# An RWKV-7 attention and a SoLU feed-forward in one kernel: GpSimd's scalings tied to points in ScalarE's work, a negated norm, shorter inverses, and a later centring of w_out

## The chip, the cores and the metric

The kernel runs on one core of a Trainium2 chip. Its time is device microseconds from the first to the last instruction of one launch with what lies around it. Three runs were timed without the profiler; the profile is of one further execution. A change is read against the median of the timed runs.

The core has five engines with a queue each, which take their instructions strictly in order: PE (TensorE: matmuls and transposes, and its weight loads, PEld), DVE (VectorE), ACT (ScalarE), POOL (GpSimd) and SP (SyncE, which here only issues transfers). ACT and POOL issue transfers too, from their own queues.

## The reference

```python
# attention, for each of 4 x 8 heads; the state is 40 x 40; 768 steps
y[:, :, t] = np.einsum('bhd,bhde->bhe', rt, state)
Sa = np.einsum('bhde,bhe->bhd', state, at)
state = state * wt[:, :, None, :] - np.einsum('bhd,bhe->bhde', Sa, bt) + np.einsum('bhd,bhe->bhde', vt, kt)

# feed-forward, on the 3072 x 320 matrix that the attention leaves
h = x @ w_in                                    # 320 -> 1024
e = np.exp(h - h_max)
solu = h * (e / (np.sum(e) + 1e-09))
ln = (solu - mu) / np.sqrt(var + 1e-06) * g_ln  # mu, var over the 1024
out = ln @ w_out                                # 1024 -> 320
```

The weights come as 64-bit floats, which the kernel takes apart by integer operations.

## The kernel before

**Tiles and slots.** The sequence is cut into chunks of 64 steps; two of the four batches go together, so there are N = 24 pieces of work (12 chunks, 2 pairs), numbered i. The main loop (line 815) runs over slots i = -1 to 27. A slot has work for several pieces at different stages: the preparation of j = i + 5 (`front`, `front_b`, `norm`: 64 x 64 matrices of a against b), the attention of i, and the feed-forward of earlier pieces (m = i - 1; `hidden(m-2)`, `output(m-3)`). Before the loop a hand-written preamble prepares pieces 0 to 3 and most of 4. The order on every engine is the order in which the program is written.

**The inverse.** Within a chunk the recurrence over 64 steps is solved with the inverse of a unit triangular matrix. `norm(j)` builds the matrix `nt` (DVE masks it out of PSUM, L375) and stores it to DRAM from POOL (L401). For every second piece `begin_inverse` starts one inverse for two pieces (16 heads each): `invert` clears a tile `uu` on POOL (L418, L419), loads the blocks of `nt` as `blk` with four POOL transfers (L412), and then yields; DVE goes on with L422 (the tile is the negative of every second row of `blk`), L423 (ones on the diagonal) and thirty steps, each a product (L428) and a subtraction (L430) on small tiles. `some(n)` and `narrow(.., n)` run n such steps at four places of a slot (`shares`). At the end the inverse goes to DRAM (L436), and `bring` (L449, L451) loads it for each piece as `tu` and `uh`. `flip` (DVE, L457) transposes a part of `tu`; then `couple` on PE makes `py` from it, which ACT copies as `wy` with the factor -1 in the lower half (L469), and `close` makes `pz`.

**Masks.** DVE masks four results of PE in a slot, from PSUM: `psi` and `lv` at its start (after `solved` and `scores`), `nt` and `lu` in its middle, all on L375; between them comes `aT` (L366).

**GpSimd's scalings.** `scaled(j+1)` multiplies b and k of piece j + 1 by the inverse decay (L337, two instructions of 128 x 320). It stands behind `flip` and `highest` in the program, but POOL goes ahead as soon as its queue allows. In front of it in POOL's queue are the loads of r (L280) and the update of the state (L638), behind it the six transfers of `left` (L648, L650), then the store of `nt` (L401), `rs` (L701) and, in every second slot, the start of an inverse.

**The mean of w_out.** The layer norm's mean is taken out of the weights once: `mean_of` (PE, L229) sums the rows of `w2` in slots 2 and 3 as its parts arrive, and `centred(mean)` (DVE, L236, two instructions) subtracts it from `w2` in slot 4, before the first half of the first `output`.

**Other places that the change touches.** In `leave` the state's new value is added up by DVE (L634); for the first piece of each pair, in slots 0 and 1, it is a copy (L636). In the preamble `decay(5)` (ACT logarithm L316, a PE matmul L325, two ACT exponentials) stands behind `some(14)`, which ends the first inverse and issues its store, and behind `scores(0)`.

Of the kernel before, what the change touches and what calls it, by code (L numbers as in the profile page):

```python
# [10 lines left out]
I32 = mybir.dt.int32  # L11
# [17 lines left out]
def shape_constants():  # L29
    s, t = np.arange(P)[:, None], np.arange(P)[None, :]  # L30
    same = s // C == t // C
    row = np.arange(P)[:, None] % C
    parts = dict(
        ident=np.eye(P),
        cum=same & (s <= t),
        tri=row < np.arange(C)[None, :],
        eye_hi=row == Q + np.arange(Q)[None, :],
        neg_hi=-(row >= Q).astype(np.float64),
        mean=np.full((P, P), 2.0 ** -10),
    )  # L40
# [8 lines left out]
def kernel(  # L49
# [46 lines left out]
    def c_(name):  # L96
        lo, hi = where[name]
        return cst[:, lo:hi]
# [124 lines left out]

    def mean_of(lo, hi, begun=None):
        t = bank("pmean")
        if begun is not None:
            nc.tensor.matmul(t[:, 0:DM], lhsT=ident, rhs=begun, start=True, stop=False)
        for c in range(lo, hi):
            nc.tensor.matmul(t[:, 0:DM], lhsT=c_("mean"), rhs=w2[:, c, :], start=begun is None and c == lo, stop=c == hi - 1)  # L229
        mean = two.tile([P, DM], FP32, tag="osb", name="mean", bufs=1)  # L230
        nc.scalar.copy(out=mean, in_=t[:, 0:DM])
        return mean

    def centred(mean):
        for x in range(0, NF, NF // 2):
            nc.vector.tensor_tensor(out=w2[:, x:x + NF // 2], in0=w2[:, x:x + NF // 2],  # L236
                                    in1=mean.unsqueeze(1).to_broadcast([P, NF // 2, DM]), op=ALU.subtract)
# [92 lines left out]
    def scaled(i, names="bk"):  # L330
# [4 lines left out]
        for n in names:  # L335
            j = H * (n == "b")
            nc.gpsimd.tensor_tensor(out=kb[:, j:j + H, 0:D], in0=d["raw_" + n], in1=heads(d["inv"]), op=ALU.mult)  # L337

    def turned(name, x):
        t = bank("p" + name)  # L340
        for j in range(4):
            nc.tensor.transpose(out=t[0:W2, j * P:(j + 1) * P],  # L342
                                in_=x[:, 2 * j:2 * j + 2].rearrange("p a b -> p (a b)")[:, 0:W2], identity=ident)
        return t[0:W2].rearrange("p (j b t) -> p b j t", j=4, b=2)
# [3 lines left out]

    def kept(name, t, bufs=1):
        o = tokens(name, bufs)  # L350
        nc.scalar.copy(out=o[0:W2], in_=t)
        return o
# [15 lines left out]
    def front_b(i):  # L368
        if not ok(i):
            return  # L370
        d = st[i]
        d["bT"] = kept("bT", turned("b", d["kb"][:, H:]))

# [41 lines left out]
    def invert(n):  # L415
        u = two.tile([P, Q // 2, Q], FP32, tag="uu", name="uu")
        flat = u.rearrange("p c t -> p (c t)")
        nc.gpsimd.memset(u[C:P], 0.0)  # L418
        nc.gpsimd.memset(flat[C:P, 1::Q + 2], 1.0)  # L419
        nb = spread(n)  # L420
        yield
        nc.vector.tensor_scalar(out=u[0:C], in0=nb[0:C, 0::2], scalar1=-1.0, scalar2=None, op0=ALU.mult)  # L422
        nc.vector.memset(flat[0:C, 0::Q + 2], 1.0)  # L423
        for j in range(1, Q - 1):
            m, n_c = Q - 1 - j, (j + 1) // 2
            prod = two.tile([P, Q * Q // 8], FP32, tag="prod", name="prod", bufs=1)
# [3 lines left out]
            nc.vector.tensor_tensor(out=u[:, 0:n_c, j + 1:Q], in0=u[:, 0:n_c, j + 1:Q], in1=t, op=ALU.subtract)  # L430
# [28 lines left out]
    def couple(i):  # L459
# [4 lines left out]
        for u in in_turn(lambda p, q, g, h: (p ^ h, p)):  # L464
# [4 lines left out]
        nc.scalar.activation(out=wy[:, :, :, 0:Q], in_=t[:, :, 0:4 * Q].rearrange("p h (j c) -> p h j c", j=4),  # L469
                             func=AF.Copy, scale=c_("neg_hi"))  # L470

# [138 lines left out]
    def leave(i):  # L610
# [21 lines left out]
        for q in range(2):  # L632
            if ci:
                nc.vector.tensor_tensor(out=tot[0:W2, q::2], in0=y[:, q, :, C:], in1=old[:, q::2], op=ALU.add)  # L634
            else:
                nc.vector.tensor_copy(out=tot[0:W2, q::2], in_=y[:, q, :, C:])  # L636
            to3 = lambda x: x[:, q::2].rearrange("p (b g) d -> p b g d", b=2)
# [48 lines left out]
    def spreadof(i):  # L686
# [4 lines left out]
        for x in range(2):  # L691
            nc.vector.bn_stats(out=bs[:, x], in_=d["e"][:, x * 512:x * 512 + 512])
        mv = small.tile([P, 2], FP32, tag="mv", name="mv")
        nc.vector.bn_aggr(out=mv, in_=bs)
# [20 lines left out]
    def output(i, x):  # L715
        if not ok(i):
            return
        d = st[i]
        bp, ci = where_(i)
# [4 lines left out]
        if x == 0:  # L724
            return
        osb = two.tile([P, DM], FP32, tag="osb", name="osb", bufs=1)
        nc.scalar.activation(out=osb, in_=d["out"][:, 0:DM], func=AF.Copy, scale=d["rs"])  # L727
        nc.scalar.dma_start(out=out.rearrange("(b s) n -> b s n", b=B)[2 * bp:2 * bp + 2, ci * C:ci * C + C], in_=osb)
# [62 lines left out]
    attend_kv(0)  # L791
    attend_r(0)
    scaled(4, "b")
    scaled(2, "k")
# [6 lines left out]
    scores(0)  # L801
    decay(5)
    load_values(1)
# [11 lines left out]
    for i in range(-1, N + 3 + LAG):  # L815
# [5 lines left out]
        if i >= 0:  # L821
            load_values(i + 2)
        narrow(0, pieces[0])

        solved(i)
        if i >= 0:
            scores(i + 1)
        if i >= 0:
            load_keys(j + 3, "w")
# [4 lines left out]
        hidden(m - 2, ((0, 1),))  # L834
        if i == 3 + LAG:
            centred(mean)
        narrow(some_weights[1], pieces[1])
# [6 lines left out]
        highest(m - 2)  # L844
        scaled(j + 1)
        left(i - 1)
# [4 lines left out]
        couple(i + 1)  # L851
        exped(m - 2)
        norm(j)
        answered(i)
# [6 lines left out]
        if i == 1 + LAG:  # L861
            mean = mean_of(0, 4)
        if i == 2 + LAG:
            mean = mean_of(4, 6, mean)
        output(m - 3, 1)

        close(i + 1)
        read(i, True)
        carried(i + 1)
        narrow(some_weights[2], pieces[3], ok(j) and j % GRP == GRP - 1)  # L870
        by_value(i + 2)
# [12 lines left out]
        if i == 2 + LAG:  # L884
            mean = mean_of(6, NF, mean)

# [29 lines left out]
```

## Time and profile before

| what | value |
|---|---|
| timed runs | 622.2, 620.62, 624.19 us; median 622.2 |
| the profiled execution | 617.47 us, its span 615.7 us |
| busy in the span | PE 547.3, DVE 448.7, ACT 265.6, POOL 257.7 us |
| DVE products and subtractions of the inverses (L428, L430) | 97.6 and 102.1 us, 360 each |
| DVE masks (L375) | four kinds, 24 each, 680 to 690 ns each |
| POOL scalings (L337) of b and of k | 24 each, 881 and 897 ns |
| POOL loads of `blk` (L412) | 46, 802 ns of issue each, 4.4 us from issue to landing |
| DVE L422; L636; L236 | 12 at 411 ns; 4 at 315 ns; 2 at 1481 ns |
| granted TensorE clock, mean over the span | 0.938 of full speed |

How to read it: busy time adds up what an engine executed; it does not say who waited. The chain that ended last is followed backwards from the last instruction; the share of an engine in it is the time in which that engine set the pace. The view by windows gives the busy time of each engine in a stretch of the span. The view in order of time shows single instructions, with the idle time before one and what ended it in brackets.

Slots by the first `solved` matmul (`pu`) in the trace: slot 0 at 63.9 us, 1 at 89.6, 2 at 108.7, 3 at 136.5, 4 at 160.4, 5 at 182.1, 6 at 204.8, and then one every 21.5 to 22.5 us up to slot 18 at 464.3.

### The profile page before, as it was taken

Reading aid. Unit: us, or ns where it says so; the run is one execution under the profiler, and the core shown is the slowest. Engines: PE = TensorE matmul, PEld = TensorE weight load, DVE = VectorE, ACT = ScalarE, POOL = GpSimd, SP = SyncE. Lnnn points to the kernel's source line nnn. Section 1 sums busy time; section 2 is a strip of 40 time slices with the busy share of each in tenths; the row PEclk is TensorE's granted clock in tenths of the full one; section 3 lists DMA queues with packets and bytes.
Section 4 is the critical chain, followed back from the end, with each engine's and each line's share of the span. In section 5 each row is a group of like instructions: output and inputs, shape, how many; then the busy total and the mean of one; then the engine's idle time right before and its main releaser. Section 6 shows DMA issues by size and latency. Waiting matters only on the chain.

```text
span 615.7 us, 26656 instructions
## 1 busy us (share of the span) xinstructions
PE 547.3 (89%) x11453; PEld 397.4 (65%) x11453; DVE 448.7 (73%) x1262; ACT 265.6 (43%) x548; POOL 257.7 (42%) x424
## 2 busy tenths in 40 slices
PE   4555587689899999999999999999999999999994
PEld 3334476566576777777777677777777676676652
DVE  4797978979968869868868868688698688443431
ACT  4434455454443544454454445444433343342221
POOL 3462272472452472473365355534624631322200
PEclk9666767789999999999999999999999999999998
DMA  8986895664445454564565574564532612310100
GB/s 166 156 157 132 176 176 107 139 137 84 82 105 98 94 118 94 97 118 99 94 122 97 95 127 97 111 110 82 109 56 53 122 44 44 65 35 26 28 19 21
DMA packets 213901, 59.93 MB, mean 97 GB/s; under 512 B 199120, under 2 KB 208952, under 8 KB 213784
## 3 DMA queue, kind: packets, MB, share of 16 engines
q1 hardware_dynamic: 195512, 33.78, 32.5%
q0 software_dynamic: 11568, 19.78, 13.9%
q10 hardware_dynamic: 6704, 4.67, 2.7%
q8 instruction: 90, 1.47, 1.0%
q14 instruction: 27, 0.22, 0.1%
HBM read 40.10 MB, written 13.37 MB: 87 GB/s over the span
## 4 chain that ended last, share of the span: by engine, by line
PE 71%; DVE 15%; DMA 4%; issue 3%; ACT 3%; SPq 1%; POOL 1%; ACTq 0%; DVEq 0%; POOLq 0%
PE po L723 16%; PE h L257 15%; PE pyo L257 7%; DVE prod L428 4%; DVE uu L430 4%; PE pu L257 4%; PE plnT L712 4%; PE ps L257 3%; PE px L257 3%; PE py L257 2%; PE pl L257 2%; PE pz L257 2%; PE pst L505 2%; PE pr L342 1%; PE pei L342 1%
## 5 line engine op out<-in xcount | busy, mean ns | idle before, releaser
L257 PE MATMUL h<-w_in,xT 128*128 128x512 f32 (+1 forms) x288 | 123.0, 610 | 0.0
L723 PE MATMUL po<-w,lnT 128*128 128x320 f32 x384 | 112.7, 438 | 0.5 <-ACT lnT L713 0.5
L430 DVE TENSOR_TENSOR uu<-uu,prod 128x30 f32<-128x30 f32 (+4 forms) x360 | 102.1, 284 | 12.4
L428 DVE TENSOR_TENSOR prod<-blk,uu 128x30 f32<-128x30 f32 (+4 forms) x360 | 97.6, 271 | 9.6
L723 PEld LDWEIGHTS po<-w,lnT 128*128 128x128 f32 x384 | 71.0, 190 | 32.6 <-issue 4.1
L401 POOL DMA_DIRECT2D nt_dram<-nt x20 | 18.9, 943 | 120.0 <-DVE nt L375 98.5
L375 DVE TENSOR_TENSOR psi<-ps,cst 128x512 f32<-128x512 f32 x24 | 16.6, 690 | 66.6 <-PE ps L257 66.6
L701 POOL TENSOR_TENSOR rs<-c,mhalf 128x1 f32<-128x1 f32 x24 | 13.5, 561 | 112.1 <-DVE c L700 103.2
L650 POOL DMA_DIRECT2D xT<-x x96 | 48.7, 512 | 0.0
L257 PEld LDWEIGHTS h<-w_in,xT 128*128 128x128 f32 (+1 forms) x288 | 37.4, 189 | 9.2 <-issue 8.1
L670 DVE TENSOR_REDUCE nmax<-h 128x1 f32<-128x1024 f32 x24 | 28.6, 1193 | 18.6 <-PE h L257 18.6
L412 POOL DMA_DIRECT2D blk<-nt_dram x46 | 36.6, 802 | 10.8 <-issue 6.8
L257 PE MATMUL pyo<-lv,kb 64*64 64x104 f32 x768 | 37.8, 266 | 2.2
L257 PEld LDWEIGHTS pyo<-lv,kb 64*64 64x64 f32 x768 | 23.9, 140 | 20.9 <-issue 20.8
L638 POOL TENSOR_TENSOR st<-tot,ex 104x160 f32<-104x160 f32 x44 | 21.8, 512 | 36.6 <-DVE tot L634 23.5
L257 PE MATMUL pyo<-lu,kb 64*64 64x104 f32 x768 | 36.7, 258 | 0.0
L469 ACT ACTIVATE wy<-py,cst 128x256 f32<-128x256 f32 x24 | 11.4, 473 | 56.2 <-PE py L257 56.2
L280 POOL DMA_DIRECT2D raw_r<-in_r_dram x48 | 33.9, 709 | 0.0
L727 ACT ACTIVATE osb<-po,rs 128x320 f32<-128x320 f32 x24 | 12.7, 527 | 48.5 <-PE po L723 32.9
L554 ACT COPY x<-px 128x320 f32<-128x320 f32 x24 | 10.2, 425 | 54.1 <-PE px L257 54.0
L678 ACT ACTIVATE e<-h,nmax 128x1024 f32<-128x1024 f32 x24 | 26.6, 1108 | 14.3 <-DVE nmax L670 14.3
L684 DVE TENSOR_TENSOR e<-h,e 128x1024 f32<-128x1024 f32 x24 | 29.2, 1217 | 4.6 <-ACT e L678 4.6
(128 smaller groups left out, 1162.6 us busy)
## 6 DMA issues: line engine op xcount, KB each, us to landing
blk<-nt_dram POOLq DMA_DIRECT2D x46, 128.0 KB, 4.4
nt_dram<-nt POOLq DMA_DIRECT2D x20, 256.0 KB, 3.5
raw_w<-in_w_dram SPq DMA_DIRECT2D x48, 80.0 KB
a<-in_a_dram SPq DMA_DIRECT2D x48, 80.0 KB
raw_r<-in_r_dram POOLq DMA_DIRECT2D x48, 80.0 KB, 3.1
lv<-in_v_dram SPq DMA_DIRECT2D x48, 80.0 KB
out_dram<-osb ACTq DMA_DIRECT2D x24, 160.0 KB
raw_b<-in_b_dram SPq DMA_DIRECT2D x44, 80.0 KB
```

The lines of the kernel that those rows point to most:

```text
L257: nc.tensor.matmul(o, lhsT=lhsT, rhs=rhs, start=start, stop=stop, skip_group_check=True)
L280: queue.dma_start(out=x[half(p), :, 0:D], in_=ap[2 * bp + p, :, ci * C:(ci + 1) * C, :].rearrange("h t d -> t h d"))
L412: queue.dma_start(out=nb[home:home + Q], in_=blocks[n][:, Q * e:Q * e + Q, Q * e:Q * e + Q])
L428: nc.vector.tensor_tensor(out=t, in0=nb[:, j:j + 1, j + 1:Q].to_broadcast([P, n_c, m]), in1=u[:, 0:n_c, j:j + 1].to_broadcast([P, n_c, m]) ...
L430: nc.vector.tensor_tensor(out=u[:, 0:n_c, j + 1:Q], in0=u[:, 0:n_c, j + 1:Q], in1=t, op=ALU.subtract)
L638: nc.gpsimd.tensor_tensor(out=to3(old), in0=to3(tot[0:W2]), in1=ex[:, :, 2 * q:2 * q + 2, C:].to_broadcast([W2, 2, 2, D]), op=ALU.mult)
L650: nc.gpsimd.dma_start(out=xT[to:to + Q, 2], in_=x[at + P - 3 * D:at + D, 2])
L670: nc.vector.tensor_reduce(out=nmax, in_=d["h"], axis=AX.X, op=ALU.max, negate=True)
L678: nc.scalar.activation(out=e, in_=d["h"], func=AF.Exp, bias=d["nmax"], accum_out=d["esum"])
L684: nc.vector.tensor_tensor(out=d["e"], in0=d["h"], in1=d["e"], op=ALU.mult)
L712: nc.tensor.transpose(out=t[:, j * P:(j + 1) * P], in_=d["e"][:, f * P:(f + 1) * P], identity=ident)
L723: nc.tensor.matmul(d["out"][:, 0:DM], lhsT=d["lnT"][:, f, :], rhs=w2[:, f, :], start=f == 0, stop=f == NF - 1)
```

## The change

- The norm is kept negated: `front_b` writes `bT` with the factor -1, `wy` gets the factor +1 (`hi`), and the steps of the inverse add. The start of the tile `uu` is then a plain copy of rows of `blk`: for the first inverse DVE copies it, for the others two more POOL transfers load it from DRAM, behind the four of `blk`.
- Steps 1 and 2 of each inverse, which have one row of products, are one DVE instruction each (`scalar_tensor_tensor`) in place of two.
- In the loop, b of piece j + 1 is scaled on POOL behind a copy of one element of `lu` (`paced`), which waits until ACT has written `lu` in `solved`; k of piece j is scaled behind a copy of one element of `wy`, before the store of `nt`. So k comes one slot later than before.
- `decay(5)` stands before the end of the first inverse.
- The copy of L636 goes from DVE to ACT.
- `mean` is a tile of its own; `centred` runs at the start of slot 5 in place of the middle of slot 4; the one output made by then, piece 0, gets its mean by `less_mean`: two DVE instructions on the result, then ACT's scaling and the store, which come behind `carried` in slot 4.

```diff
-        neg_hi=-(row >= Q).astype(np.float64),
+        hi=(row >= Q).astype(np.float64),
...
-        mean = two.tile([P, DM], FP32, tag="osb", name="mean", bufs=1)
+    mean = const.tile([P, DM], FP32, name="mean")
...
+    pace = const.tile([1, 1], FP32, name="pace")
+
+    def paced(x):
+        nc.gpsimd.tensor_copy(out=pace, in_=x)
...
-    def kept(name, t, bufs=1):
+    def kept(name, t, bufs=1, sign=1.0):
         o = tokens(name, bufs)
-        nc.scalar.copy(out=o[0:W2], in_=t)
+        nc.scalar.mul(out=o[0:W2], in_=t, mul=sign) if sign != 1.0 else nc.scalar.copy(out=o[0:W2], in_=t)
...
-        d["bT"] = kept("bT", turned("b", d["kb"][:, H:]))
+        d["bT"] = kept("bT", turned("b", d["kb"][:, H:]), sign=-1.0)
...
         nb = spread(n)
+        if n:
+            for e in range(2):
+                nc.gpsimd.dma_start(out=u[Q * e:Q * e + Q], in_=blocks[n][:, Q * e:Q * e + Q:2, Q * e:Q * e + Q])
         yield
-        nc.vector.tensor_scalar(out=u[0:C], in0=nb[0:C, 0::2], scalar1=-1.0, scalar2=None, op0=ALU.mult)
+        if not n:
+            nc.vector.tensor_copy(out=u[0:C], in_=nb[0:C, 0::2])
         nc.vector.memset(flat[0:C, 0::Q + 2], 1.0)
         for j in range(1, Q - 1):
             m, n_c = Q - 1 - j, (j + 1) // 2
+            if n_c == 1:
+                nc.vector.scalar_tensor_tensor(out=u[:, 0, j + 1:Q], in0=nb[:, j, j + 1:Q], scalar=u[:, 0, j:j + 1],
+                                               in1=u[:, 0, j + 1:Q], op0=ALU.mult, op1=ALU.add)
+                yield
+                continue
...
-            nc.vector.tensor_tensor(out=u[:, 0:n_c, j + 1:Q], in0=u[:, 0:n_c, j + 1:Q], in1=t, op=ALU.subtract)
+            nc.vector.tensor_tensor(out=u[:, 0:n_c, j + 1:Q], in0=u[:, 0:n_c, j + 1:Q], in1=t, op=ALU.add)
...
-                             func=AF.Copy, scale=c_("neg_hi"))
+                             func=AF.Copy, scale=c_("hi"))
...
-                nc.vector.tensor_copy(out=tot[0:W2, q::2], in_=y[:, q, :, C:])
+                nc.scalar.copy(out=tot[0:W2, q::2], in_=y[:, q, :, C:])
...
+        if x and i:
+            sent(i, d["out"][:, 0:DM])
+
+    def less_mean(i):
+        d = st[i]
+        mu = small.tile([P, 1], FP32, tag="mu", name="mu")
+        nc.vector.tensor_scalar(out=mu, in0=d["mv"][:, 0:1], scalar1=-1.0 * DFF, scalar2=None, op0=ALU.mult)
+        t = two.tile([P, 512], I32, tag="scale", name="scale").bitcast(FP32)[:, 0:DM]
+        nc.vector.scalar_tensor_tensor(out=t, in0=mean, scalar=mu, in1=d["out"][:, 0:DM], op0=ALU.mult, op1=ALU.add)
+        sent(i, t)
+
+    def sent(i, x):
...
         osb = two.tile([P, DM], FP32, tag="osb", name="osb", bufs=1)
-        nc.scalar.activation(out=osb, in_=d["out"][:, 0:DM], func=AF.Copy, scale=d["rs"])
+        nc.scalar.activation(out=osb, in_=x, func=AF.Copy, scale=d["rs"])
...
     attend_r(0)
+    decay(5)
     scaled(4, "b")
...
     scores(0)
-    decay(5)
...
         narrow(0, pieces[0])
+        if i == 4 + LAG:
+            centred()
         solved(i)
         if i >= 0:
             scores(i + 1)
-        if i >= 0:
+            if ok(j + 1):
+                paced(st[i]["lu"][0:1, 0, C:C + 1])
+                scaled(j + 1, "b")
             load_keys(j + 3, "w")
...
-        if i == 3 + LAG:
-            centred(mean)
...
-        scaled(j + 1)
         left(i - 1)
...
         exped(m - 2)
+        if i < 0:
+            scaled(j + 1, "b")
+        elif ok(j):
+            paced(wy[0:1, 0, 0, 0:1])
+            scaled(j, "k")
         norm(j)
...
         carried(i + 1)
+        if m - 3 == 0:
+            less_mean(0)
```

More of the change, by code (lines that the diff above doesn't have):

```diff
@@ L221, in turn_g, with mean_of, centred @@
             nc.scalar.mul(out=x, in_=pg[:, 0:NF], mul=2.0 ** y)
-    def mean_of(lo, hi, begun=None):
+    mean = const.tile([P, DM], FP32, name="mean")
+    def mean_of(lo, hi):
         t = bank("pmean")
-        if begun is not None:
-            nc.tensor.matmul(t[:, 0:DM], lhsT=ident, rhs=begun, start=True, stop=False)
+        if lo:
+            nc.tensor.matmul(t[:, 0:DM], lhsT=ident, rhs=mean, start=True, stop=False)
         for c in range(lo, hi):
-            nc.tensor.matmul(t[:, 0:DM], lhsT=c_("mean"), rhs=w2[:, c, :], start=begun is None and c == lo, stop=c == hi - 1)
-        mean = two.tile([P, DM], FP32, tag="osb", name="mean", bufs=1)
+            nc.tensor.matmul(t[:, 0:DM], lhsT=c_("mean"), rhs=w2[:, c, :], start=c == 0, stop=c == hi - 1)
         nc.scalar.copy(out=mean, in_=t[:, 0:DM])
-        return mean
-    def centred(mean):
+    def centred():
         for x in range(0, NF, NF // 2):
@@ L692, in spreadof @@
             nc.vector.bn_stats(out=bs[:, x], in_=d["e"][:, x * 512:x * 512 + 512])
-        mv = small.tile([P, 2], FP32, tag="mv", name="mv")
+        mv = d["mv"] = small.tile([P, 2], FP32, tag="mv", name="mv")
         nc.vector.bn_aggr(out=mv, in_=bs)
@@ L718, in output @@
         d = st[i]
-        bp, ci = where_(i)
         if x == 0:
@@ L723, in output @@
             nc.tensor.matmul(d["out"][:, 0:DM], lhsT=d["lnT"][:, f, :], rhs=w2[:, f, :], start=f == 0, stop=f == NF - 1)
-        if x == 0:
-            return
+        if x and i:
[8 more added lines that the diff above has]
+    def sent(i, x):
+        d = st[i]
+        bp, ci = where_(i)
         osb = two.tile([P, DM], FP32, tag="osb", name="osb", bufs=1)
-        nc.scalar.activation(out=osb, in_=d["out"][:, 0:DM], func=AF.Copy, scale=d["rs"])
+        nc.scalar.activation(out=osb, in_=x, func=AF.Copy, scale=d["rs"])
         nc.scalar.dma_start(out=out.rearrange("(b s) n -> b s n", b=B)[2 * bp:2 * bp + 2, ci * C:ci * C + C], in_=osb)
@@ L861 @@
         if i == 1 + LAG:
-            mean = mean_of(0, 4)
+            mean_of(0, 4)
         if i == 2 + LAG:
-            mean = mean_of(4, 6, mean)
+            mean_of(4, 6)
         output(m - 3, 1)
@@ L884 @@
         if i == 2 + LAG:
-            mean = mean_of(6, NF, mean)
+            mean_of(6, NF)
 _INS = ['r', 'k', 'v', 'w', 'a', 'b', 'moe_w_in', 'moe_w_out', 'moe_g_ln']
```

## The prediction

> **What bounds the kernel now.** I read the page's slices, then the view by windows, then the view in order of time where an instruction lasts longer than its like.
>
> ```profile
> PE   4555587689899999999999999999999999999994
> ...
> DVE  4797978979968869868868868688698688443431
> ...
> PEclk9666767789999999999999999999999999999998
> ```
>
> The first quarter is another kernel than the rest. In it DVE is the full engine; later PE is.
>
> ```profile
> core 0: us, PE busy (x) PEld busy (x) DVE busy (x) ACT busy (x) POOL busy (x), PEclk, DMA share, GB/s
> 26.00:49.00 23.00, 10.34 (x126) 7.16 (x124) 20.97 (x66) 5.27 (x11) 13.94 (x20) 0.57 0.83 154
> ...
> 109.00:132.00 23.00, 18.06 (x443) 13.15 (x436) 19.80 (x56) 11.00 (x24) 13.01 (x21) 0.78 0.67 142
> 132.00:160.40 28.40, 23.70 (x497) 16.39 (x496) 26.12 (x68) 14.82 (x31) 13.31 (x21) 1.00 0.44 89
> ...
> 182.10:464.30 282.20, 278.20 (x6269) 205.08 (x6268) 220.50 (x640) 129.48 (x270) 135.69 (x220) 1.00 0.53 101
> 464.30:505.20 40.90, 39.38 (x917) 28.69 (x916) 31.19 (x96) 16.29 (x33) 16.41 (x30) 1.00 0.37 72
> ```
>
> From 182 to 464 PE is busy 278.20 of 282.20 us at full clock: whatever DVE, ACT or POOL save there is worth nothing while no wait of PE appears. In 464-505 PE lacks 1.5 us. Up to 160 DVE is busy 85 to 92% and PE waits for it. So the change is worth what it takes from DVE before 160 us, less what it adds on PE's waits later.
>
> The view in order of time shows what the pacing is about.
>
> ```profile
> 119.68 2.17 DVE L430 TENSOR_TENSOR uu<-uu,prod 128x84 f32<-128x84 f32 x1
> ...
> 120.05 0.87 POOL L337 TENSOR_TENSOR kb<-raw_b,inv 128x320 f32<-128x320 f32 x1
> ...
> 120.87 0.87 POOL L337 TENSOR_TENSOR kb<-raw_k,inv 128x320 f32<-128x320 f32 x1
> ...
> 122.34 4.48 PE L229 MATMUL pmean<-w,cst 128*128 128x320 f32 x8
> ```
>
> A subtraction that takes 0.24 us elsewhere took 2.17 and ended as POOL's second scaling did. A DVE mask beside a scaling keeps its 0.68 (79.15, k at 79.23). Between 26 and 160 us I find 14.1 us of such excess on DVE, about 0.6 per scaling that meets a step of an inverse (63.02: 0.90 against 0.28). This is what can be won, but only where DVE sets the pace.
>
> **The change part by part**, against the profiled execution.
>
> *Preamble.* Two steps of the inverse become one instruction each: four of 0.19, issued every 0.225, give way to two. The trace has no scalar_tensor_tensor of 30 elements; its nearest rows are 0.16 (128x1) and 0.48 (128x320); I take 0.22, so 0.45 is saved per inverse. k of piece 4 meets the last subtraction at 48.13 (0.80 against 0.18). Two more loads now stand before it on POOL: each between 0.51 (an xT transfer) and 0.80 (`blk`), 1.0 to 1.6 together, so it falls among masks: -0.62. Together -1.07 at the first inverse's store (48.96). decay(5) moved up frees PE for `pa`, so `aT` comes 3 us earlier; but the next thing is `flip` at 57.13, which needs the inverse back from DRAM (stored at 48.96, last load issued 54.3-54.9), and DVE then waits for the new loads of the second inverse (issued until about 49.5, landing 4.4 later) where L422 stood at 53.87. Taken: -0.9, bounds -0.7 and -1.1.
>
> *Slot -1.* k of piece 5 moves away from the step at 65.87: -0.57.
>
> *Slot 0.* b now waits for `lu` (66.6), then for its own load, issued at 68.4-70.2: it lands among the steps of 71.3-74.1, +0.6. The stall at 76.80 (1.36 against 0.24) goes, but `lu`'s mask (79.75) waits for PE's `pl` (to 79.46), so only 0.3 of it counts. k behind `wy` (78.3) falls beside `nt`'s mask, free. Net +0.3, bounds 0 and +0.6. The copy L636 goes to ACT (nearest rows 0.18 for 128x8, 0.43 for 128x320; 0.3 each): DVE gains 0.46, ACT's next instruction (86.53) 0.3 of it; bounds 0 and -0.46.
>
> *Slot 1.* L422 (0.41) and the two steps (0.45) go, the loads having landed by about 92 for 94.8: -0.86. k behind `wy` (99.97) meets the steps of 100.0-100.9: +0.6; before, b and k ran at 91.1-92.8 while DVE idled 3.47. L636: -0.46. Net -0.7, bounds -1.3 and -0.2.
>
> *Slot 2.* b follows `lu` and POOL's state update and r loads, so about 112.9, where steps end and masks begin (113.14): +0.2, bounds 0 and 0.6. The 1.93 us stall shown above vanishes, worth nothing: PE's `pmean` (122.34-126.82) and ACT's weight work behind it end later.
>
> *Slot 3.* Stalls of 1.86 and 0.60 at 134.85 and 137.12 vanish; PE's `ps` ends at 138.49 and the mask began at 138.71, so 0.2 counts. L422 and two steps: -0.86; k behind `wy` (145.1) on steps: +0.6. Net -0.46, bounds -1.06 and 0.
>
> Sum to slot 4: -0.9 - 0.57 + 0.3 - 0.3 - 0.7 + 0.2 - 0.46 = -2.4.
>
> *Slots 4 to 17: nothing.* Centring (2.88) leaves slot 4, where PE was never idle, and goes to slot 5, where DVE idles 5.15 before `psi` (185.34); without that cover it would be 2.9 on `aT` and so on PE. less_mean is 0.10 plus between 0.16 and 0.69 on DVE, in place of 2.88. The negations ride on ACT (0.597 for a scaled copy, 0.582 for a plain one). A pace copy costs POOL 0.10 to 0.56; behind it queue b, six xT transfers, k, the store of `nt` and `rs`. Their users are a slot away or, for the store, DVE's mask is later (302.48 against `wy` at 300.73 + 0.9). k meets steps at 300.8-301.7 and pushes `lu`'s mask to 303.7; PE uses it at 304.84.
>
> *Slot 18.* Here PE does wait:
>
> ```profile
> 492.12 0.45 DVE L457 STREAM_TRANSPOSE tu<-tu 128x256 f32<-128x256 f32 x1 [0.79 <-DMA tu<-uu_dram]
> ```
>
> `flip` waits for an inverse whose last steps DVE finished at 481.5, in a slot without other idle time on DVE. No b is left to take away, but k of piece 23 behind `wy` (472.96) meets steps: +0.6, bounds 0 and 0.9, straight onto PE's wait of 1.18.
>
> Total -2.4 + 0.6 = -1.8: the span 615.7 becomes 613.9. The profiled run (617.47) is 4.7 below the median of the timed ones, which I take to shift alike: 622.2 - 1.8 = 620.4. The bounds add to -4.8 and +0.6.
>
> One rule is at odds with the rows. The Trainium skill, "SBUF — State Buffer", section "Who interferes with whom", says that of a DVE instruction with two SBUF inputs and a GpSimd one that reads SBUF, whichever issues first holds the shared port and the other blocks. At 119.68 DVE was first by the record and still paid 1.93. By the rule some of my three +0.6 for k would fall on POOL, which has time: about 0.9 less, 619.5. The same page (section "SBUF: two separate sides") says that DVE's two-port instructions hold up the descriptors of POOL's transfers, which speaks against two more of them; at 80.68 it was DVE that paid (0.79 against 0.42, beside a POOL store), and no such instruction runs where the new loads are issued, so I add nothing.
>
> **The rivals.**
>
> *Slower: the new loads land late.* In odd slots DVE reached L422 at 316.67, flipped at 319.56, and PE took `py` at 321.04. The loads end their issue near 312.8; `flip` can follow a landing by 2.04, lasts 0.44, so PE waits from a landing after 318.56, 5.8 us after issue. `blk` takes 4.4 in the median, but an inverse's store took 5.29 in the chain. At 6.5 us, eight odd slots lose 0.7 each: 5.6 - 1.8, so 626.0. Decides from 5.8 us. 10%.
>
> *Faster: the ramp's clock.* The granted clock is 0.57 to 0.78 until 132 us and 1.00 after. If a denser ramp brings full clock to slot 2, eight `pmean` matmuls take 2.5 (four took 1.24 at 146.41) for 4.48, and `py`, `pnt`, `pl` 2.0 for 3.3: -3.3 - 1.8, 617.1. For it: PE waits less. Against: 2 us in 130 is little. With my own gains at their upper bounds it comes to the same time. 36%.
>
> *The stall only moves.* b and k meet steps in all four ramp slots: +0.6 for k in slots 0 and 2, for b in 1 and 3, +0.4 in 2: +2.8, so 623.2; against it, masks follow `lu` closely in slots 1 and 3. 12%.
>
> **How the numbers follow.** Forecast 42%: 620.4. About 0.5% (3.1 us) is what a measurement here can tell from no change. Slower 0.10; faster 0.36 plus 0.02 from the forecast's edge, 0.38; within 0.52. The range reaches from below the clock's case to above the moved stall's, 616.0 to 624.0; the late loads lie outside, and their 10% with the far ends makes the two in ten.
>
> **What would show it.** Right: `flip` of slot 0 near 56.2, slot 4's `pu` near 158.0 instead of 160.4, slots from 5 on as long as before, no subtraction above 1 us in slots 2 and 3, PE's wait in slot 19 grown to 1.8. Wrong: a wait of L423's memset for `uu`'s loads followed by PE idle at `py`; a slot length other than 21.5; scalings still beside steps.

## The result, and the profile after

| | before | changed |
|---|---|---|
| first group of runs, median (lowest to highest) | 622.27 us (620.62 to 624.19, 4 runs) | 627.97 us (626.78 to 633.7, 4 runs) |
| ratio, 95% interval | | 1.0119 (1.0083 to 1.0156) |
| second group, median | 621.27 us (26 runs) | 626.02 us (623.51 to 629.37, 7 runs) |
| ratio, 95% interval | | 1.0070 (1.0041 to 1.0099) |
| profiled execution | 617.47 us, span 615.7 | 626.78 us, span 625.0 |

The change makes the kernel 0.7 to 1.2% slower. Line numbers after it: masks L382, loads of `uu` L430, memset L434, steps L444 and L446, `flip` L473, `wy` L485, store of `nt` L408, `blk` L419, `tot` on ScalarE L652, `x` L635.

The slices of the changed kernel's page, same three engines as before:

```profile
PE   5564588788999999999999999999999899999994
...
DVE  4796969679778749768958877688688468433431
...
PEclk9665765699999998999999999999999989999998
```

VectorE's busy time fell from 448.7 to 438.7 us, so the change took off VectorE what it was written to take off. But PE's row has an 8 at three quarters, and the clock's row an 8 among the nines in two places. The windows show the same (time, then busy time of each engine, granted clock, DMA):

```profile
core 0: us, PE busy (x) PEld busy (x) DVE busy (x) ACT busy (x) POOL busy (x), PEclk, DMA share, GB/s
...
109.00:132.00 23.00, 18.89 (x402) 14.46 (x406) 16.81 (x51) 11.23 (x25) 11.15 (x21) 0.69 0.59 120
132.00:161.54 29.54, 25.09 (x554) 17.61 (x546) 25.30 (x72) 16.25 (x34) 15.60 (x26) 1.00 0.58 104
182.97:468.43 285.46, 280.27 (x6265) 206.13 (x6264) 217.13 (x620) 129.75 (x270) 149.59 (x260) 0.99 0.57 104
468.43:514.33 45.90, 42.67 (x914) 30.78 (x913) 31.46 (x93) 16.33 (x33) 19.92 (x36) 0.93 0.38 70
```

The stretch from slot 5 to slot 18 took 285.46 us for 282.20, and the one from 18 to 20 took 45.90 for 40.90, at a clock of 0.93. These two are most of the loss. First `pu` matmul of some slots, with a second profile of the same kernel beside it:

| slot | before | changed | changed, second profile |
|---|---|---|---|
| 1 | 89.59 | 88.97 | 89.72 |
| 2 | 108.71 | 111.47 | 112.02 |
| 4 | 160.38 | 161.54 | 162.59 |
| 7 | 226.52 | 227.54 | 228.57 |
| 8 | 248.14 | 252.14 | 250.45 |
| 17 | 443.31 | 447.46 | 445.60 |
| 18 | 464.27 | 468.43 | 468.86 |
| 19 | 485.00 | 489.44 | 489.88 |
| 20 | 505.16 | 514.33 | 515.74 |

So three places lose: slot 1 (22.5 and 22.3 us for 19.1), one odd slot in the middle (slot 7 in one profile, 24.6 us for 21.6, slot 17 in the other, 23.3 for 21.0), and slot 19 (24.9 and 25.9 for 20.2). A slot from 5 on that is 2 us or more longer than in the kernel before, behind a wait of TensorE for `flip`, is called a long slot below; `flip`'s part is shown next. From slot 20 on, both kernels take 110.5 to 110.7 us.

Slot 7 of the changed kernel in order of time (start, length, engine, line, idle time before it and what ended it):

```profile
218.02 0.96 POOL L408 DMA_DIRECT2D nt_dram<-nt  x1 [1.55 <-DVE nt L382]
...
223.78 3.18 POOL L419 DMA_DIRECT2D blk<-nt_dram  x4 [0.94 <-DMA nt_dram<-nt]
226.96 1.29 POOL L430 DMA_DIRECT2D uu<-nt_dram  x2
...
234.57 0.07 DVE L434 MEMSET uu<- 64x16 f32 x1 [2.98 <-DMA xT<-x]
...
236.77 0.44 DVE L473 STREAM_TRANSPOSE tu<-tu 128x256 f32<-128x256 f32 x1
...
237.26 0.67 PE L257 MATMUL py<-tu,nt 64*64 64x32 f32 x32 [1.32 <-DVE tu L473]
```

The store of `nt` is issued at 218.02 and has not landed when POOL reaches `blk`, which waits 0.94 us for it. Behind `blk` come the two loads of `uu`, issued until 228.25. VectorE's memset, which needs them, starts at 234.57 after 2.98 us of idleness; eight short instructions of the inverse stand behind it and then `flip`, for which TensorE's `py` waits 1.32 us. (The label names the transfer `xT`; in odd slots with a shorter wait, as 322.07, it names `uu<-nt_dram`. In every kernel below that lacks these loads this wait is gone.) Then the clock goes, as the windows behind it show:

```profile
237.00:239.00 2.00, 1.63 (x95) 1.50 (x96) 1.93 (x5) 1.00 (x2) 0.39 (x2) 1.00 0.76 125
239.00:241.00 2.00, 2.00 (x20) 1.38 (x13) 1.83 (x6) 0.57 (x2) 0.61 (x1) 0.61 0.72 124
241.00:243.00 2.00, 2.00 (x5) 1.02 (x4) 2.00 (x4) 0.00 (x0) 0.89 (x1) 0.54 0.01 3
243.00:245.00 2.00, 2.00 (x102) 1.77 (x101) 1.93 (x4) 1.10 (x3) 0.07 (x1) 1.00 0.57 129
```

From 239.43 to 242.85, 3.41 us, the granted clock is 0.50. TensorE is busy all that time; if it gets half as much done, that is 1.7 us by estimate, and with the wait of 1.3 this makes the 3.0 us that slot 7 loses. In slot 19 of the second profile it is worse, the same chain in VectorE's and TensorE's lines:

```profile
497.51 0.07 DVE L434 MEMSET uu<- 64x16 f32 x1 [4.18 <-DMA xT<-x]
...
499.71 0.44 DVE L473 STREAM_TRANSPOSE tu<-tu 128x256 f32<-128x256 f32 x1
...
500.30 1.08 PE L257 MATMUL py<-tu,nt 64*64 64x32 f32 x32 [3.85 <-DVE tu L473]
```

Why the store of `nt` is late is in slot 10, which is typical, in VectorE's and POOL's lines of the changed kernel:

```profile
304.88 0.22 POOL L344 COPY pace<-wy 1x1 f32<-1x1 f32 x1 [3.36 <-ACT wy L485]
305.06 0.85 POOL L337 TENSOR_TENSOR kb<-raw_k,inv 128x320 f32<-128x320 f32 x1
305.09 0.93 DVE L446 TENSOR_TENSOR uu<-uu,prod 128x84 f32<-128x84 f32 x1
306.49 0.68 DVE L382 TENSOR_TENSOR nt<-pnt,cst 128x512 f32<-128x512 f32 x1
307.47 0.97 POOL L408 DMA_DIRECT2D nt_dram<-nt  x1 [1.55 <-DVE nt L382]
```

The same step and the same mask in the kernel before:

```profile
301.08 0.25 DVE L430 TENSOR_TENSOR uu<-uu,prod 128x84 f32<-128x84 f32 x1
...
301.80 0.68 DVE L375 TENSOR_TENSOR nt<-pnt,cst 128x512 f32<-128x512 f32 x1
```

k, released by `wy`, falls on a step that stands just ahead of the mask of `nt`: 0.93 us for 0.25. Measured from the `pu` of the odd slot that follows, that mask ends 9.54 us ahead here, in slots 9 to 15 alike, and in the kernel before 10.23 ahead in slots 9, 11 and 15 and 10.56 in slot 13.

The third place is slot 1, on ScalarE, first the changed kernel, whose `tot` is there now, with VectorE's `x` above it and TensorE's `pr` below:

```profile
108.62 0.76 DVE L635 TENSOR_TENSOR x<-pyo,ex 104x256 f32<-104x256 f32 x2
...
109.41 0.49 ACT L652 COPY tot<-pyo 104x160 f32<-104x160 f32 x2 [2.09 <-DVE x L635]
109.79 0.60 ACT L358 COPY kT<-pk 104x512 f32<-104x512 f32 x1
...
110.44 1.10 PE L349 MATMUL pr<-cst,r 128*104 128x128 f32 x4 [1.73 <-ACT kT L358]
```

then the same place with `tot` on VectorE again (experiment e2):

```profile
108.51 0.59 ACT L358 COPY kT<-pk 104x512 f32<-104x512 f32 x1 [0.57 <-PE pk L349]
...
109.23 0.75 DVE L635 TENSOR_TENSOR x<-pyo,ex 104x256 f32<-104x256 f32 x2
109.91 0.54 DVE L652 COPY tot<-pyo 104x160 f32<-104x160 f32 x2
```

ScalarE's `tot` starts when VectorE's `x` has ended, and `kT`, which needs neither, stands behind it in ScalarE's queue. TensorE's `pr` waited 1.73 us for that `kT`, and slot 2's `pu` came after it. In the five profiles with `tot` on ScalarE slot 1 takes 21.7 to 23.2 us, in the thirteen with it on VectorE 18.2 to 21.3.

### The profile page after: what moved, and what is told of

Its sections match the earlier page's. It is cut to its first block, busy times and chain, and to the rows that moved or that the text cites. A ratio compares the mean times of both kernels' runs of the same rounds, so it can differ in the third digit from the quotient of the medians.

```text
span 625.0 us, 26681 instructions
## 1 busy us (share of the span) xinstructions
PE 558.8 (89%) x11453; PEld 406.4 (65%) x11453; DVE 438.7 (70%) x1225; ACT 266.8 (43%) x552; POOL 279.4 (45%) x483
## 4 chain that ended last, share of the span: by engine, by line
PE 66%; DVE 18%; DMA 6%; issue 4%; ACT 3%; POOL 2%; SPq 1%; ACTq 0%; DVEq 0%
PE po L738 15%; PE h L257 14%; PE pyo L257 6%; DVE prod L444 5%; DVE uu L446 5%; PE pu L257 4%; PE ps L257 3%; PE plnT L728 3%; PE px L257 3%; PE py L257 2%; PE pl L257 2%; DMA nt_dram<-nt 2%; PE pz L257 2%; PE pr L349 2%; PE pst L521 2%
## 5 line engine op out<-in xcount | busy, mean ns | idle before, releaser
L738 PE MATMUL po<-w,lnT 128*128 128x320 f32 x384 | 116.6, 450 | 0.5 <-ACT lnT L729 0.5
L446 DVE TENSOR_TENSOR uu<-uu,prod 128x56 f32<-128x56 f32 (+7 forms) x336 | 95.7, 285 | 11.5
L444 DVE TENSOR_TENSOR prod<-blk,uu 128x56 f32<-128x56 f32 (+7 forms) x336 | 91.1, 271 | 9.2
L738 PEld LDWEIGHTS po<-w,lnT 128*128 128x128 f32 x384 | 72.9, 195 | 34.1 <-issue 6.4
L382 DVE TENSOR_TENSOR psi<-ps,cst 128x512 f32<-128x512 f32 x24 | 16.6, 691 | 72.6 <-PE ps L257 72.6
L419 POOL DMA_DIRECT2D blk<-nt_dram x46 | 36.6, 802 | 11.7 <-DMA nt_dram<-nt 6.3
L485 ACT ACTIVATE wy<-py,cst 128x256 f32<-128x256 f32 x24 | 11.4, 474 | 56.0 <-PE py L257 55.9
L337 POOL TENSOR_TENSOR kb<-raw_b,inv 128x320 f32<-128x320 f32 x24 | 20.7, 864 | 29.9 <-DMA raw_b<-in_b_dram 20.9
```

The source lines that it names most:

```text
L419: queue.dma_start(out=nb[home:home + Q], in_=blocks[n][:, Q * e:Q * e + Q, Q * e:Q * e + Q])
```

## The experiments

All runs were timed in five rounds beside the kernel before (26 to 35 runs of it in each group), and each ratio is taken within its group. The first group holds e1, e2, e3 and e6, the second the changed kernel again, e4, e7 and e8, the third e9 to e12, the fourth e13 to e16. "pu 4" is the profile's time of slot 4's first `pu`, "4 to 20" the time from it to slot 20's.

| label | pacing of b, k | start of `uu` | `tot` | ratio, 95% interval | pu 4 | 4 to 20 |
|---|---|---|---|---|---|---|
| before | none | DVE | DVE | 1 | 160.38 | 344.8 |
| changed, second group | `lu`, `wy` | loads | ACT | 1.0070 (1.0041 to 1.0099) | 162.59 | 353.2 |
| e1 | `lu`, `wy` | DVE | ACT | 1.0057 (1.0032 to 1.0082) | 166.69 | 347.7 |
| e2 | `lu`, `wy` | loads | DVE | 1.0060 (1.0030 to 1.0090) | 159.27 | 357.0 |
| e3 | `lu`, `wy` | DVE | DVE | 1.0015 (0.9993 to 1.0037) | 163.57 | 347.3 |
| e6 | none | loads | ACT | 1.0024 (1.0000 to 1.0049) | 163.93 | 346.6 |
| e4 | none | loads | DVE | 0.9984 (0.9965 to 1.0003) | 161.25 | 347.2 |
| e7 | none | DVE | DVE | 0.9951 (0.9932 to 0.9971) | 161.91 | 346.2 |
| e10 | none | loads | DVE | 0.9964 (0.9936 to 0.9991) | 160.16 | 345.0 |
| e11 (e7, decay back) | none | DVE | DVE | 0.9939 (0.9914 to 0.9964) | 161.35 | 347.0 |
| e12 (e7, centring back) | none | DVE | DVE | 0.9959 (0.9937 to 0.9981) | 160.86 | 344.8 |
| e8 | `lu`, behind store | DVE | DVE | 0.9993 (0.9972 to 1.0015) | 163.04 | 347.0 |
| e9 | `lu`, behind store | loads | DVE | 0.9978 (0.9953 to 1.0002) | 161.29 | 345.7 |
| e15 | `lu`, behind store | loads | ACT | 1.0008 (0.9987 to 1.0029) | 162.32 | 347.0 |
| e13 | none, behind store | DVE | DVE | 0.9986 (0.9965 to 1.0006) | 160.61 | 344.4 |
| e16 (e13, decay back) | none, behind store | DVE | DVE | 0.9988 (0.9964 to 1.0012) | 162.34 | 345.1 |
| e14 | `lu`, none | DVE | DVE | 1.0008 (0.9987 to 1.0028) | 162.70 | 345.2 |

e4 has besides neither the centring in slot 5 nor the earlier decay.

**The two suspects one by one and together, and the pacing.** e1 drops the loads of `uu`; e2 puts `tot` back; e3 does both; e6 takes the pacing out and leaves both.

```diff
 # e1, e3
         nb = spread(n)
-        if n:
-            for e in range(2):
-                nc.gpsimd.dma_start(out=u[Q * e:Q * e + Q], in_=blocks[n][:, Q * e:Q * e + Q:2, Q * e:Q * e + Q])
         yield
-        if not n:
-            nc.vector.tensor_copy(out=u[0:C], in_=nb[0:C, 0::2])
+        nc.vector.tensor_copy(out=u[0:C], in_=nb[0:C, 0::2])
 # e2, e3
-                nc.scalar.copy(out=tot[0:W2, q::2], in_=y[:, q, :, C:])
+                nc.vector.tensor_copy(out=tot[0:W2, q::2], in_=y[:, q, :, C:])
 # e6
-            if ok(j + 1):
-                paced(st[i]["lu"][0:1, 0, C:C + 1])
-                scaled(j + 1, "b")
...
         highest(m - 2)
+        scaled(j + 1)
         left(i - 1)
...
-        if i < 0:
-            scaled(j + 1, "b")
-        elif ok(j):
-            paced(wy[0:1, 0, 0, 0:1])
-            scaled(j, "k")
         norm(j)
```

> The changed kernel, but each inverse starts from a VectorE copy of blk (as inverse 0 does) and the two loads of uu are not issued. Theory A (the loads of uu land about 6.3 us after their issue, hold the memset and with it flip and py, and the idle TensorE then loses its clock): the waits before slot 8's and slot 20's pu go, slots 7 and 19 are 21.6 and 20.2 us again instead of 24.6 and 24.9, so about 7.7 us less than the changed kernel's 628: 620 to 622, with the ramp's +1.2 us still there (and up to 0.4 us more per copy in slots 1 and 3). Rival C (the pacing itself: k beside steps and the later store of nt): the slots 7 and 19 stay long, 626 to 629.

> The changed kernel, but the first state's copy (tot, slots 0 and 1) is on VectorE again. Theory B (ScalarE's tot waits 2.1 us for VectorE's x and holds kT behind it, so pu of slot 2 starts late): slot 2's pu comes 2 us earlier against slot 1's flip, slot 4's pu at 159 to 160 instead of 161.5, and the time about 1.5 to 2.5 us below the changed kernel's 628, with the long slots left where loads land late. Rival: ScalarE's order is not what holds slot 2 (pnt's or pl's slow clock is); then slot 4's pu stays at 161.5.

> Both of these: no loads of uu, and tot on VectorE. If A and B are separate causes that add, 618 to 620, a little below the kernel before (622.3). If only A holds, 620 to 622; if only B, 625 to 627.

> The changed kernel without the pacing: b and k are scaled together after flip, as in the kernel before; the loads of uu stay. Theory A with the loads alone as cause: VectorE's memset still waits in odd slots, 624 to 628. If the later store of nt (the pacing, 0.7 us in slot 6) is needed to bring the loads over the edge: slots 7 and 19 are 21.6 and about 21 us, and the time is 620 to 623. The ramp pays the scalings beside steps again (up to 2 us).

e1 and e3 have no long slot: slot 7 takes 21.9 and 21.5 us, slot 19 21.2 and 21.1. The stretch from 4 to 20 is 5 to 6 us shorter than in the changed kernel. So without the loads no slot is long. Slot 19 still has a wait for `flip` (2.17 and 0.77 us), and `blk` waits 1.05 and 1.01 us for the store there. In times both came out worse than expected: the ramp (the time before slot 4) takes its share, and e1's profile has the slowest of all. e2 has slots 17 and 19 long (25.9 and 24.0), and its slot 4 begins at 159.27 as expected, 2.3 us earlier than the changed kernel's first profile; with two long slots its time is only 0.1% below the changed kernel's second group (0.6% below the first). The times show the loads less clearly than the profiles: e1 is within the changed kernel's interval of the second group, and e3 is 0.45% below e2, with intervals that just overlap. `tot` costs 0.42% between e1 and e3. e6 has both halves of the answer: its loads are issued 0.69 us earlier than the changed kernel's, end 0.27 us before `pu` of the odd slots instead of 0.43 after it, the memset waits 0.3 to 0.5 us in four slots, and TensorE never waits for `flip` before slot 20. So it takes both to make a long slot: the loads, and k behind `wy`, which makes the store later.

**The changed kernel again, the inverse alone, the rest alone, k elsewhere.** e4 is the kernel before with negation, fused steps and loads. e7 is e3 without the pacing. e8 is e3 with k moved:

```diff
-        elif ok(j):
-            paced(wy[0:1, 0, 0, 0:1])
-            scaled(j, "k")
         norm(j)
+        if i >= 0 and ok(j):
+            scaled(j, "k")
```

> The changed kernel unaltered, for a second profile and for times beside the kernels of this group. If the late loads depend on the luck of their landing, the long slots move: one to three of the eight odd slots from 5 to 19 are 3 to 5 us too long, not necessarily slots 7 and 19 alone (19 is the likeliest, its loads are issued 1.2 us later than those of the other slots). If something fixed in slot 7 makes it long, it is 24.6 us again. Ratio to the kernel before 1.009 to 1.014.

> The kernel before with the inverse's part alone: negated norm, first steps fused, and the two loads of uu; no pacing, no other move. Theory A with the pacing as its second half: the loads end their issue about 0.3 us before pu of the odd slots, as in the kernel without pacing, so flip is at 6.0 to 7.6 us after pu and TensorE never waits for it but in slot 19; late part as in the kernel before, ramp 0.5 to 1 us shorter: ratio 0.997 to 1.002. Rival (the loads alone suffice): 1.004 to 1.010.

> The changed kernel without its three suspects: no pacing, no loads of uu (a VectorE copy instead), the first tot on VectorE. What is left of the change: the fused steps, the negated norm, decay 5 earlier, the centring in slot 5. If the three suspects are the whole loss, 0.997 to 1.001. If the centring or the earlier decay costs too, 1.003 or more.

> No loads of uu, tot on VectorE, b paced on lu as in the changed kernel, but k is scaled behind the issue of the norm's store instead of behind wy. Theory: the 0.69 us by which nt's mask is later in the odd slots (9.54 instead of 10.23 us before pu) is k's doing alone; nt's mask is back at 10.2 us, blk no longer waits 1.0 us for the store in slot 19, and TensorE's wait there falls from 2.2 and 0.8 us to 0 to 0.5. Ratio 0.997 to 1.001, against 1.0015 with k behind wy. Rival (b's pacing makes the mask late): the mask stays at 9.54 and the ratio at 1.0015.

In the changed kernel's second profile the long slots moved, to 17 and 19; slot 7 took 21.88 us. So which slot is long changes from one execution to the next, by how long the transfers take to land, with slot 19 the likeliest. The ratio, 1.0070, is below the 1.009 to 1.014 expected. e4 shows that the loads alone make no long slot. e7 is faster than was expected of it: what is left of the change beats the kernel before by 0.5%. In e8 the mask of `nt` is back at 10.23 us, and `blk` waits for no store. But TensorE still waited 1.73 us for `flip` in slot 19, so a late store is not the only thing that makes `flip` late there, and slot 15 took 24.8 us behind a wait of 1.33 us that the profile puts down to nothing that it shows, with the clock at half behind it. Such waits stand inside `ps`, the matmuls of `scores`, in most profiles, paced or not: 0.83 us in slot 5 of the kernel before, 1.44 in slot 19 of e7. What they wait for is open.

**Loads with k elsewhere, loads without pacing, the two small moves.** e9 is e2 with k behind the store; e10 is e6 with `tot` on VectorE; e11 is e7 with `decay(5)` back behind `scores(0)`; e12 is e7 with `centred()` back in slot 4 and without `less_mean`.

> The changed kernel with its loads of uu and b paced on lu, tot on VectorE, but k scaled behind the issue of the norm's store. Theory (the loads hurt because k behind wy makes them 0.69 us later): their issue ends 0.3 us before pu of slots 7 to 17 instead of 0.4 behind it, flip stays below 8.2 us after pu there, and the ratio is 0.998 to 1.002, against 1.006 with k behind wy. Rival (two loads more on the queue suffice, whenever k runs): long slots as in the changed kernel, 1.004 to 1.008.

> The version without pacing, with tot on VectorE, and with the loads of uu instead of the VectorE copy. If the loads cost nothing without pacing: the same as the version with the copy (0.9951), 0.993 to 0.998, and no wait of py for flip above 0.5 us before slot 20. If they cost by themselves: 0.999 or more.

> The version without the three suspects (0.9951), with decay 5 back where it stood. If the earlier decay is worth something (aT of slot -1 came 3 us earlier, but the prediction put it behind flip's wait), 0.997 or more; if nothing, 0.994 to 0.997.

> The version without the three suspects (0.9951), with the centring back in slot 4 and no correction of output 0. Slot 4 was 21.71 us in the kernel before and 21.43 where the centring is in slot 5; so about 0.3 us, 0.05%, is what the profiles show: 0.995 to 0.997, not told apart by the times, but by slot 4 (21.7) and slot 5 (22.5 or more).

e9 against e2 is one edit and 0.8%: 0.9978 for 1.0060. Its lines where the changed kernel's were shown above:

```profile
303.81 0.24 DVE L446 TENSOR_TENSOR uu<-uu,prod 128x78 f32<-128x78 f32 x1
303.97 0.68 DVE L382 TENSOR_TENSOR nt<-pnt,cst 128x512 f32<-128x512 f32 x1
...
304.95 0.93 POOL L408 DMA_DIRECT2D nt_dram<-nt  x1 [5.33 <-DVE nt L382]
305.90 0.89 POOL L337 TENSOR_TENSOR kb<-raw_k,inv 128x320 f32<-128x320 f32 x1
```

No step stands beside k, and k's 0.89 us lie in the time in which the store is under way. The loads end their issue 0.24 us before `pu`, and no slot from 5 to 19 is long by a wait for `flip`. (Slot 9 took 23.55 us: a wait of 1.78 us, again put down to nothing.) e10 agrees with e7: without pacing, loads or copy are the same. Its one wait in slot 19 was 1.78 us, more than expected. e11, at 0.9939, is a hair below the range that was expected if the earlier decay brings nothing, and its interval overlaps e7's: the times tell no worth of it. e12 shows the 0.2 to 0.3 us in slot 4 (21.64 for 21.43), too little for the times.

**What the pacing costs by itself, and the changed kernel mended.** e13 is e7 with k behind the store, e14 is e7 with b behind `lu`, e16 is e13 with the decay back, and e15 is the changed kernel with the k edit alone.

> The version without the three suspects (0.9951), but k scaled behind the issue of the norm's store; b where it was in the kernel before. In the two profiles with k there, the excess of VectorE's steps from 160 to 500 us fell from 9 us to below 1, in slots in which TensorE sets the pace. If b behind lu is what made that version slower than the one without pacing (0.9993 against 0.9951): 0.992 to 0.997. If k behind the store costs: 0.998 to 1.001.

> The same version with b paced on lu and k at its old place behind flip. If b behind lu costs: 0.998 to 1.001; if not: 0.993 to 0.997.

> The changed kernel with one edit: k is scaled behind the issue of the norm's store and not behind wy; loads of uu, b on lu, tot on ScalarE stay. Theory: no long slots but perhaps slot 19; what is left is the wait of ScalarE's tot in slots 0 and 1 (0.4 to 0.6%): 1.001 to 1.005, against 1.007 to 1.012. Rival (the long slots have another cause): 1.006 or more.

> The first of these with decay 5 back where it stood. The decay alone made no difference that the times tell (0.9939 against 0.9951): 0.992 to 0.997, and the best of all if k behind the store is worth something by itself.

e15 shows that moving k alone takes the changed kernel from 1.0070 to 1.0008: 0.6%, with intervals that do not meet. Its slots from 4 to 17 are all between 21.2 and 22.8 us; slot 19 took 22.3, behind a wait of 1.42 us put down to nothing, with the clock at half. `tot` on ScalarE is the 0.3% between e15 and e9, with overlapping intervals. e13, e14 and e16 miss the hope set on them: with either scaling moved the kernel is 0.3 to 0.6% slower than without, whichever of the two it is, and e16 is not the best version. For k (e13 against e7, e16 against e11) the intervals still touch, for b (e14 against e7) they do not. Where this goes is not settled: from slot 4 to 20 these three take no longer than e7, so it may be the ramp, but there single profiles do not repeat well enough: slot 4 begins at 160.2 to 161.9 in the four without pacing, at 160.6 to 163.0 in e8, e13, e14 and e16.

The best version is e11, or any of e7, e10 and e12, whose intervals overlap: negated norm and fused first steps, no pacing, `tot` on VectorE: 617.76 us for 621.21, ratio 0.9939 (0.9914 to 0.9964).

## Why the prediction was wrong

The forecast was 620.4 us with 0.6 us lost from slot 4 on and 2.4 us won before it. Measured were 627.97 us, above the range. The two profiles differ by 9.3 us, the medians by 5.7 and 4.8, so some 4 us of what the profiles show is the luck of single executions.

- **The step that failed: "Slots 4 to 17: nothing."** It holds the right observation, that k meets steps at 300.8-301.7, and follows it to `lu`'s mask alone: "pushes `lu`'s mask to 303.7; PE uses it at 304.84". For the store it kept the mask of `nt` at 302.48, although that mask stands directly ahead of `lu`'s on VectorE and is pushed with it. Behind the mask of `nt` hang the store, `blk`, the new loads, the memset and `flip` of the next slot. The mask ends 0.69 us later, and where the transfers then land slowly the delay reaches TensorE. From slot 4 to slot 18 that cost 3.0 and 2.4 us where nothing was forecast; from slot 18 to slot 20 the same path has the larger part of 5.0 and 6.0 us for the 0.6 forecast.
- **The late loads were the rival at 10%.** Its condition was right: the sign named as "wrong", a memset waiting for `uu` and then TensorE idle at `py`, is what appeared. It was priced wrongly on two counts. It put the end of the loads' issue at 312.8, 0.1 us behind slot 11's `pu`, and left out that the change's own pacing moves the store on which they hang. It was 0.43 behind `pu` in most odd slots, but 0.7 to 1.7 in all six long slots of three profiles (two each in both profiles of the changed kernel and in e2): in these, and in no other odd slot of theirs from 5 on, `blk` waited 0.94 to 1.45 us for the store of `nt` to land. The landing itself was slower too: the second load landed 4.8 to 6.2 us after the end of its issue in the long slots, 3.6 to 5.4 in the other odd slots from 7 on. Without k behind `wy` the loads make no long slot (e4, e9, e10, e15). And it spread 0.7 us over eight slots; two of them lost 2.3 to 5.7 each, in five of the six because the clock goes with the wait (slot 17 of the second profile kept it). 626.0 was still near the measured time, by errors that cancel.
- **The pacing did not take the stalls off VectorE in the late slots.** Counted as each step's time above the lower quartile of its line and form, steps from 160 to 500 us paid 8.9 us too much before and 9.0 after. Before, b and k met two steps at the end of every second slot (289.86, 290.72), and TensorE did not wait behind them; after, k meets one in nearly every slot just ahead of `nt`'s mask. Behind the store it is 0.4 and 0.5 us (e8, e9). Nor are these stalls worth anything by themselves: e7 pays 9.6 us there and is among the fastest, e14 pays 0.4 and is slower. In the ramp the stalls did fall, from 10.0 to 6.2 us from 26 to 160 us, and the 1.93 us at 119.68 is gone, as forecast.
- **Ramp: +1.2 and +2.2 us for -2.4.** The term "L636: -0.46" in slot 1 was of the wrong sign. ScalarE's queue was costed at 0.3 per copy, but the copy also waits 2.09 us for VectorE's `x`, and `kT` behind it; over three pairs of kernels (e1 and e3, e6 and e10, e15 and e9) that is 0.3 to 0.6%, 1.9 to 3.7 us. In the fourth pair, the changed kernel and e2, it is 0.1%, and in e2's profile two long slots cost what the ramp gained.
- **Preamble.** k(4) no longer stands on the last subtraction (0.18 for 0.80 us) and `aT` comes at 49.42 for 52.59, as forecast. But the time went into a wait for ScalarE's `scale`, which the prediction left out, as VectorE's lines in the changed kernel show, and `flip` came at 56.56 (57.34 in the second profile) for 57.13: 0.57 or nothing of the 0.9. A fused step, taken at 0.22 us, took 0.27 (51.59, two in 0.54).

```profile
49.42 0.68 DVE L373 TENSOR_TENSOR aT<-pa,ex 104x512 f32<-104x512 f32 x1
...
54.62 0.69 DVE L193 SCALAR_TENSOR_TENSOR bits<-bits,scale 128x512 int32<-128x512 int32 x1 [2.49 <-ACT scale L185]
...
56.56 0.44 DVE L473 STREAM_TRANSPOSE tu<-tu 128x256 f32<-128x256 f32 x1
```

- **The clock in the ramp** was the rival with 36%, and went the other way: from 90 to 110 us it was granted 0.50 for 0.77 before. TensorE was busy 17.04 us for 15.55 there, but at a lower clock the same matmuls keep it busy for longer (the 32 of `py`: 1.08 us at 500.30, at half clock, for 0.67 at 237.26). No experiment controlled it; in the other profiles it was 0.50 to 0.74, and 0.51 in e10, one of the fastest.
- **Slot 18 and 19: +0.6.** The direction was right: the wait for `flip` was 2.38 and 3.85 us for 1.18, and the slot 4.7 and 5.7 us longer. That k by itself adds to the wait is not shown: without the loads it was 2.17 and 0.77 us (e1, e3), and with k behind the store besides still 1.73 (e8). In slot 19 the loads end their issue 1.7 and 1.5 us after `pu`, for 0.4 in most odd slots.
- **The baseline.** The profiled execution before was taken to stand to its median as the others would. In the ramp it was a quick one: slot 4 began at 160.4, in the sixteen experiments at 159.3 to 166.7.
- **A slip in the sum.** The lower bounds of the items add to -4.5 us, not to -4.8; neither the forecast nor the range rests on it.
- **Right:** slots without a late load stayed near 21.5 us; the centring costs nothing in slot 5; no subtraction above 1 us was left in slots 2 and 3; the decay was worth nothing.

The Trainium skill, "TensorE: Matmul & The Clock Gate", section "HAM oscillation — how this bites in real kernels", gives as a rule that TensorE should have no idle gaps above some 3.4 us. The rows here are stricter: behind gaps of 1.32 us (slot 7) and 2.38 us (slot 19) the granted clock was at half for 3.41 and 6.83 us, so by the rule slot 7 would have lost 1.3 us where it lost 3.0. The same page's Part 1 says that the window which is watched runs freely, so that the moment of a change depends on where in it the activity falls. The traces agree in that within a run all changes of the granted clock lie on one grid of 3.41 us, whose offset differs from run to run; and the gap of 1.78 us in e10, which kept the clock at 1.00, is split by a point of that grid (491.9). But where a gap falls does not settle it alone: the 1.83 us in the changed kernel's second profile (453.46 to 455.29) lay within one stretch of the grid, 452.05 to 455.46, and the clock stayed at 1.00.

## What to carry to other kernels

When an engine's work is moved next to another engine, follow every user of every instruction that gets later, down to the next transfer, and not only the first one that is seen to be late: here a stalled step was harmless by way of the one mask whose user was followed, and made two slots long by way of the mask beside it and a store. A transfer that replaces a 0.4 us instruction is only free while its landing is ahead by more than landings vary; and a copy moved to an idle engine takes its waits into that engine's queue. Prices on TensorE's waits should count the clock: here a wait of 1.32 us cost 3.0, since 3.41 us at half clock came behind it.

## What the runs showed of the hardware

TensorE's granted clock fell to half behind waits of 1.32 and 2.38 us (changed kernel, slots 7 and 19), 3.85 (its second profile, slot 19), 2.06 and 1.92 (e2, slots 17 and 19), 1.33 (e8, slot 15) and 1.42 us (e15, slot 19). It stayed at 1.00 behind waits of 1.32 (e6, slot 5), 1.71 (e11, slot 19), 1.73 (e8, slot 19), 1.78 (e9, slot 9, and e10, slot 19), 1.83 (second profile, slot 17) and 2.17 us (e1, slot 19). So from 1.3 us on the length of the wait alone does not decide. The half clock lasted 3.41 or 6.83 us each time. In slot 7 of the changed kernel it is this stretch, between two at full clock:

```profile
236.02:239.43 3.41, 2.06 (x97) 1.86 (x98) 3.24 (x9) 1.43 (x3) 0.82 (x2) 1.00 0.76 127
239.43:242.85 3.42, 3.42 (x8) 2.04 (x7) 3.25 (x9) 0.14 (x2) 0.92 (x2) 0.50 0.31 52
242.85:246.26 3.41, 3.41 (x134) 2.56 (x132) 3.20 (x10) 1.62 (x4) 0.78 (x2) 1.00 0.41 94
```

And e10 across its wait of 1.78 us, which kept the clock:

```profile
491.00:493.00 2.00, 0.32 (x21) 0.35 (x25) 1.31 (x4) 0.00 (x0) 0.00 (x0) 1.00 0.61 98
493.00:495.00 2.00, 2.00 (x61) 1.62 (x55) 1.83 (x7) 1.57 (x3) 0.00 (x0) 1.00 0.04 8
495.00:497.00 2.00, 2.00 (x63) 1.40 (x65) 1.93 (x5) 0.53 (x1) 0.00 (x0) 1.00 0.00 0
```

The landing of the same loads also varied, with nothing changed in the kernel: in the two profiles of the changed kernel the memset of slot 7 waited 2.98 and 0.35 us, that of slot 17 not at all and 2.94.
